# The spectrum of each kernel step as two row tiles of 64 rows, copied out in two halves, with a new order of the whole program

## The chip, the cores and the metric

The kernel runs on one core of one Trainium2 chip. The metric is the device time of one execution in microseconds (us), as a median over several executions. The engines of a core work side by side, each through its own instructions in a fixed order: TensorE (PE in the profile, with its weight loads as PEld), VectorE (DVE), ScalarE (ACT), GpSimd (POOL), and SyncE (SP), which issues most of the transfers.

## The reference

The reference runs two rounds of two layers on 2048 tokens of 512 channels. The first layer is a long convolution (S4D): from the parameters a kernel of 2048 taps is made for each channel, and the convolution is done by FFT. The second sends the two best-scored tokens through a feed-forward network. Cut to what matters here:

```python
def _A_ref(u, log_A_real, A_imag, C_real, C_imag, log_dt, D_skip):
    dt = jnp.exp(log_dt)
    A = -jnp.exp(log_A_real) + 1j * A_imag
    C = (C_real + 1j * C_imag) * dt[:, None]
    P = jnp.exp((A * dt[:, None])[:, :, None] * pos[None, None, :])
    K = 2.0 * jnp.einsum("dn,dnl->dl", C, P).real
    Kf = jnp.fft.rfft(K, L2)
    Uf = jnp.fft.rfft(u_t, L2)
    y = jnp.fft.irfft(Uf * Kf[None, :, :], L2)[:, :, :L]
    return y + u * D_skip[None, None, :]
...
    x = x + _A_ref(_layernorm(x, axis=-1), ...)
    x = x + _B_ref(_layernorm(x, axis=-1), ...)
    x = x + _A_ref(_layernorm(x, axis=-1), ...)
    x = x + _B_ref(_layernorm(x, axis=-1), ...)
```

## The kernel before

The 512 channels are cut into four chunks (c) of 128. The convolution kernel K of all channels is made in 32 steps u (class KStep), eight to a chunk, 16 channels to a step. The change touches the end of a step.

**One step.** ACT, POOL and DVE make the terms: ACT the phase and its sine and cosine (tiles ph and tr, lines 665, 693, 699 and 702), POOL the phase sums and the decay (ph and mg, lines 669, 683 and 688), DVE their products (sc, lines 710, 712 and 717). Then PE contracts them over the 128 states into the taps of the step (contract, L725, 32 matmuls in four column tiles of 32 columns): the tile pk has 128 partitions, 32 rows a for each of four channels g, and four such groups e. ACT copies pk to SBUF as kt (taps, L729), DVE adds the skip term (skip, L732). PE makes the first stage of the spectrum (spectrum, L745): for each e, kt is the stationary operand of two matmuls (real and imaginary part) against the constant d1k of 128 columns, 32 frequencies for each of four channels. d1k is block diagonal: it holds zeros where channel and row group differ. The result kq fills one PSUM bank, and ACT copies it out (turn, L755, 512 elements per partition) into gk, the spectrum tile of the chunk, laid out as 32 frequencies by 128 channels. The copy writes runs of four neighbouring channels.

**The PSUM banks.** pk and kq share one bank (tag "pk", one buffer) in turn: the contraction of the next step waits for the turn of the one before. The bank with tag "u" (one buffer) belongs to the convolution itself: to kx of even number (kf_mm, L778, second stage of the spectrum of K) and to pu (front_mm, L778, the same stage for the input), which two products on DVE read (front_tt, L819: p<-pu,kd and p<-pu,ks).

**The stages.** From about 20 us to 280 us (times of the profile) the 32 steps run, and interleaved with them the convolution of chunks 0 to 2 in the first round: zf (L845, first stage of the input), kx, pu, pv (back_mm, L827, first inverse stage), the copy w of pv on ACT (L1102), the way of w through DRAM (vd, then v) and po (L913, last stage). The copies on ACT differ in how they lie in memory: L498 copies 128 floats into every eighth place of the tile eight (32 bytes apart), L500 pairs of 16-bit halves into the same places, L641 writes exponentials into every second place (8 bytes apart) in the set-up, and L1693, late in the program, reads 512 floats that lie 128 bytes apart, with a factor per partition.

From 280 us on there are no steps any more: chunk 3, the routed tokens (pt, pi, pr, pq, ph, then pg and pu on the weights, L1470), the second round, and the routed tokens again at the very end (from 500 us).

**What sets the order.** Each call of the program (put_in) belongs to a lane, and the table PLAN gives every call of a lane its position in one agenda. The calls are sorted by that position, and each engine runs its instructions in the order in which they were then written. A second PLAN section orders what comes after 280 us. The lines "aw" (keep_awake, L1697) are matmuls whose result nobody reads; they keep PE going where it would sit idle.

Of the kernel before, what the change touches and what calls it, by code (L numbers as in the profile page):

```python
# [42 lines left out]
    ],  # L43
    x0=[103, 57, 141, 123],
    stat0=[105, 107, 104, 110, 99, 58, 59, 97, 161, 150, 144, 142, 128, 131, 124, 125],
    phase8=[
        94, 108, 109, 112, 85, 179, 199, 240, 259, 220, 346, 354, 364, 375, 358, 456, 470, 476, 492, 478, 606, 630, 631, 633, 589,
        707, 731, 782, 783, 791, 907, 933, 934, 946, 896, 1055, 1078, 1081, 1082, 1057,
    ],
    decay8=[  # L50
        87, 117, 121, 126, 106, 207, 247, 266, 277, 214, 371, 389, 390, 391, 393, 466, 474, 505, 509, 511, 601, 602, 603, 638,
        627, 740, 774, 775, 777, 727, 901, 929, 950, 960, 895, 1095, 1096, 1100, 1108, 1161,
    ],
    phase_0=[
        114, 113, 166, 152, 260, 264, 304, 330, 376, 407, 406, 445, 493, 538, 577, 518, 647, 676, 702, 690, 784, 787, 865, 815,
        947, 970, 1020, 1033, 1133, 1165, 1225, 1085,
    ],
# [19 lines left out]
    ],  # L77
    prod_b=[
# [3 lines left out]
    ],  # L82
    prod_p=[
# [3 lines left out]
    ],  # L87
    contract=[
        140, 209, 237, 271, 316, 348, 367, 384, 420, 463, 501, 529, 565, 598, 654, 670, 715, 721, 764, 831, 871, 930, 964, 980,
        997, 1073, 1125, 1175, 1230, 1246, 1275, 1286,  # L90
    ],
    z=[153, 481, 751, 1065],
    table=[162, 163, 168, 173, 174, 180, 181, 189, 190, 191, 193, 194, 430],
    taps=[
        164, 210, 243, 278, 324, 349, 368, 386, 423, 464, 506, 531, 578, 618, 655, 671, 716, 733, 770, 849, 876, 931, 966, 981,
        1013, 1089, 1127, 1178, 1231, 1247, 1277, 1287,
    ],
    skip=[
        182, 211, 248, 281, 325, 350, 373, 388, 431, 471, 507, 542, 585, 619, 657, 672, 717, 734, 771, 860, 883, 936, 967, 988,
        1015, 1090, 1129, 1189, 1236, 1252, 1278, 1293,  # L100
    ],
    spectrum=[
        183, 230, 298, 301, 334, 355, 381, 400, 450, 489, 508, 543, 637, 649, 662, 681, 754, 951, 816, 861, 903, 941, 975, 989,
        1068, 1107, 1150, 1241, 1255, 1267, 1300, 1318,
    ],
    keep=[184, 226, 249, 282, 347, 353, 374, 432],
    turn=[
        195, 231, 300, 309, 335, 365, 383, 401, 453, 490, 521, 546, 643, 650, 663, 685, 755, 958, 817, 862, 908, 948, 976, 990,
        1072, 1112, 1152, 1242, 1256, 1273, 1307, 1320,
    ],  # L110
    norm=[
# [15 lines left out]
    params=[340, 469, 520, 684, 893, 1006],
    inv=[359],
# [1738 lines left out]
```

## Time and profile before

| | us |
|---|---|
| median of three runs | 533.95 |
| lowest and highest | 530.01 and 534.79 |
| the profiled execution | 535.15 |
| its span, first to last instruction | 533.3 |

Busy time in the profiled execution: PE 437.0 us, DVE 424.5, ACT 386.3, POOL 316.9. The profile cuts the span into stages; busy time per stage is to be read against the length of the stage. The end of a matmul is modelled, so PE's busy time is not PE at its peak. A duration is that of one instruction from start to end; instructions that follow each other on one engine overlap a little, so the distance from one start to the next is what an instruction costs an engine that is never idle. The trace puts an idle time before an instruction down to what ended it (`<-`).

### The profile page before, as it was taken

Reading aid. Unit: us, or ns where it says so; the run is one execution under the profiler, and the core shown is the slowest. Engines: PE = TensorE matmul, PEld = TensorE weight load, DVE = VectorE, ACT = ScalarE, POOL = GpSimd, SP = SyncE. Lnnn points to the kernel's source line nnn. Section 1 sums busy time; section 2 is a strip of 40 time slices with the busy share of each in tenths; the row PEclk is TensorE's granted clock in tenths of the full one; section 3 lists DMA queues with packets and bytes.
Section 4 is the critical chain, followed back from the end, with each engine's and each line's share of the span. In section 5 each row is a group of like instructions: output and inputs, shape, how many; then the busy total and the mean of one; then the engine's idle time right before and its main releaser. Section 6 shows DMA issues by size and latency. Waiting matters only on the chain. (4 is left out here: it accounts for less than half of the span.)

```text
span 533.3 us, 14085 instructions
## 1 busy us (share of the span) xinstructions
PE 437.0 (82%) x5428; PEld 341.9 (64%) x5428; DVE 424.5 (80%) x987; ACT 386.3 (72%) x862; POOL 316.9 (59%) x334
## 2 busy tenths in 40 slices
PE   1014378999999999989989985999799999989468
PEld 1013356889778887779749743766578798754235
DVE  7999987878989998999885588574457799799841
ACT  5998989999998998888714645143556867559891
POOL 0496679997978487554506824056306868987200
PEclk9999999999999999999999998799899999999769
DMA  7244988879576877767636899743574668747643
GB/s 252 98 178 132 278 310 305 250 178 256 160 214 172 222 224 249 212 142 218 198 123 197 303 398 361 292 166 116 152 268 157 192 185 256 224 163 329 237 178 140
DMA packets 67307, 115.77 MB, mean 217 GB/s; under 512 B 8708, under 2 KB 50984, under 8 KB 62504
## 3 DMA queue, kind: packets, MB, share of 16 engines
q1 hardware_dynamic: 67112, 114.85, 66.0%
q8 instruction: 43, 0.70, 0.5%
q14 instruction: 24, 0.20, 0.1%
q0 software_dynamic: 128, 0.02, 0.0%
HBM read 68.83 MB, written 39.72 MB: 204 GB/s over the span
## 5 line engine op out<-in xcount | busy, mean ns | idle before, releaser
L873 POOL TENSOR_TENSOR y<-p 64x256 f32<-64x256 f32 x76 | 58.3, 768 | 73.4 <-DVE p L858 56.6
L717 DVE TENSOR_TENSOR sc<-tr,mg 128x1024 f32<-128x1024 f32 x64 | 77.1, 1210 | 2.1 <-POOL mg L688 1.5
L725 PE MATMUL pk<-sc 128*32 128x64 f32 x2048 | 39.6, 235 | 36.6 <-DVE sc L717 28.1
L725 PEld LDWEIGHTS pk<-sc 128*32 128x32 f32 x2048 | 34.1, 119 | 47.8 <-issue 29.1
L669 POOL TENSOR_TENSOR ph<-eight,far 128x768 int32<-128x768 int32 x32 | 53.3, 1672 | 16.2 <-ACT tr L702 15.8
L845 PE MATMUL zf<-z,d 128*128 128x256 f32 x192 | 57.8, 438 | 0.2 <-DVE b L1412 0.2
L683 POOL TENSOR_TENSOR mg<-eight,far 128x768 f32<-128x768 f32 x32 | 53.5, 1672 | 7.0 <-DVE sc L712 6.3
L849 DVE STREAM_TRANSPOSE g<-zf 128x512 f32<-128x512 f32 x64 | 45.0, 709 | 15.9 <-PE zf L845 14.6
L745 PE MATMUL kq<-d1k,kt 128*64 128x128 f32 x512 | 38.5, 297 | 16.7 <-ACT rq0b L949 9.2
L1102 ACT ACTIVATE w<-pv 128x512 f32<-128x512 f32 x48 | 28.2, 590 | 32.7 <-PE pv L879 18.7
L879 PE MATMUL pv<-y,w 128*128 128x128 f32 x320 | 46.1, 286 | 4.7 <-POOL y L871 3.0
L688 POOL TENSOR_TENSOR mg<-mg,f32s 128x512 f32<-128x512 f32 x32 | 34.2, 1071 | 24.4 <-ACT mg L677 16.6
L879 PEld LDWEIGHTS pv<-y,w 128*128 128x128 f32 x320 | 39.7, 191 | 13.5 <-POOL y L871 5.1
L858 DVE TENSOR_TENSOR p<-pu,kf 128x1024 f32<-128x1024 f32 x32 | 38.9, 1222 | 10.2 <-PE pu L768 5.8
L745 PEld LDWEIGHTS kq<-d1k,kt 128*64 128x64 f32 x512 | 30.2, 147 | 24.8 <-ACT rq0b L949 9.4
L845 PEld LDWEIGHTS zf<-z,d 128*128 128x128 f32 x192 | 37.6, 213 | 11.2 <-DVE g L849 2.5
L768 PE MATMUL pu<-g,w 128*64 128x128 f32 x640 | 43.1, 278 | 0.4 <-DVE b L1449 0.3
L768 PEld LDWEIGHTS pu<-g,w 128*64 128x64 f32 x640 | 36.8, 134 | 7.1 <-issue 4.3
L871 POOL TENSOR_TENSOR y<-p 64x256 f32<-64x256 f32 x52 | 38.6, 743 | 3.2
L827 PE MATMUL pv<-p,w 128*128 128x128 f32 x192 | 38.2, 280 | 0.0
L827 PE MATMUL pv<-p,w3b 128*128 128x128 f32 x192 | 37.1, 275 | 0.0
L702 ACT ACTIVATE tr<-ph,cst 128x1024 f32<-128x1024 f32 x32 | 35.6, 1113 | 1.5 <-DVE sc L717 1.0
(380 smaller groups left out, 1138.5 us busy)
## 6 DMA issues: line engine op xcount, KB each, us to landing
vd<-w SPq DMA_DIRECT2D x48, 256.0 KB, 3.0
v<-vd SPq DMA_DIRECT2D x24, 512.0 KB, 5.7
wd<-in_wd SPq DMA_DIRECT2D x4, 2048.0 KB, 11.0
kf<-kfd SPq DMA_DIRECT2D x16, 512.0 KB, 6.7
ks<-kd SPq DMA_DIRECT2D x48, 128.0 KB, 2.8
kfd<-kd SPq DMA_DIRECT2D x24, 256.0 KB, 3.7
x<-in_xr SPq DMA_DIRECT2D x4, 1024.0 KB, 6.4
z<-in_x SPq DMA_DIRECT2D x4, 1024.0 KB, 5.4
```

The lines of the kernel that those rows point to most:

```text
L669: G.tensor_tensor(self.ph[:, :, 8:32].rearrange("p d (k i) -> p d k i", k=3), self.first(0).rearrange("p d (o i) -> p d o i", o=1).to_broa ...
L683: G.tensor_tensor(mg[:, :, 0:2, 8:32].rearrange("p d t (k i) -> p d t k i", k=3), self.first(1).rearrange("p (d t o) i -> p d t o i", t=2, ...
L717: V.tensor_tensor(sc.rearrange("p d (t i) -> p d t i", t=3)[:, :, 0:3:2, :], t, self.mg[:, :, 0:3:2, :], op=OP.mult)
L725: T.matmul(self.pk[32 * g : 32 * g + 32, e, :], t[:, 0:32], t[:, 32:96], start=k == 1, stop=k == 0, tile_position=(0, 32 * g))
L745: T.matmul(self.pq[64 * ri : 64 * ri + 64, e].rearrange("p k g -> p (k g)"), self.kt[:, e].rearrange("p h b -> p (h b)"), d1k[:, 128 * ri ...
L768: T.matmul(pt[64 * par : 64 * par + 64, ri, q, :], w2[:, k1, 64 * ri : 64 * ri + 64], col(src, k1), start=True, stop=True, tile_position=( ...
L827: T.matmul(pv[:, k, :], w[:, j, :], p[:, t, k % 2, k // 2, :], start=t == 0, stop=t == 1)
L845: T.matmul(pf[:, 16 * s : 16 * s + 16, :], d1[:, 128 * s : 128 * s + 128], z[:, :, 16 * q : 16 * q + 16], start=True, stop=True)
L849: V.transpose(g[:, :, 16 * q : 16 * q + 16, :].rearrange("p k e t -> p e k t"), pf.rearrange("p (k t) e -> p e k t", t=2))
L858: V.tensor_tensor(pp, pu.rearrange("p (o r) q e -> p o r (q e)", o=1).to_broadcast([128, 2, 2, 2 * CH]), kf.rearrange("p r (o q) e -> p r ...
L873: E.tensor_tensor(y[0:64, :, par, :], p[0][ls, 0], p[1][ls, 1], op=OP.subtract)
L879: T.matmul(pv[:, k, :], w3[:, 4 * gi + k, :], y[:, k // 2, k % 2, :], start=True, stop=True)
```

## The change

1. The spectrum is cut in two by rows. Rows 0 to 63 of kt (channels g = 0, 1) and rows 64 to 127 (g = 2, 3) are multiplied apart, each against 64 columns of d1k, which is 128 columns wide now and has lost half of its zeros. A step has 16 matmuls of 64 rows, 64 stationary and 64 moving columns, in place of 8 of 128 rows, 64 stationary and 128 moving columns.
2. The two row tiles write to different banks: the first to the bank of pk as before, the second to the bank "u".
3. The turn becomes two instructions on ACT, one for each half, of 256 elements per partition. The channels of a step are dealt to e and g in another way (contract and the layout of the skip term follow), so that a half covers eight neighbouring channels; the copy runs over the 32 frequencies innermost, and in gk neighbouring frequencies lie 128 floats apart. It therefore writes single floats 512 bytes apart.
4. The store of the taps of chunk 0 (keep) is two transfers in place of one, eight times.
5. The tables of PLAN are all new, also those of the stages after 280 us. No other instruction is added or removed, but ACT has 21 loads of its function tables in place of 20; the additional one stands in the set-up, before step 2.

```diff
@@ constants
-    d1k = np.zeros((4, 32, 2, 32, 4))
+    d1k = np.zeros((4, 32, 2, 2, 32))
     for g in range(4):
-        d1k[g, :, 0, :, g] = np.cos(th)
-        d1k[g, :, 1, :, g] = -np.sin(th)
+        d1k[g, :, 0, g % 2, :] = np.cos(th)
+        d1k[g, :, 1, g % 2, :] = -np.sin(th)
@@ contract
-                            t = self.sc[:, k, 4 * e + g, :]
+                            t = self.sc[:, k, 8 * (g // 2) + 2 * e + g % 2, :]
@@ spectrum
-                self.pq = psk.tile([128, 4, 32, 4], F32, name=f"kq{self.u}", tag="pk")
+                self.pq = [
+                    (ps if r else psk).tile([128, 4, 2, 32], F32, name=f"kq{self.u}_{r}", tag=("pk", "u")[r]) for r in range(2)
+                ]
                 for e in range(4):
-                    for ri in range(2):
-                        T.matmul(
-                            self.pq[64 * ri : 64 * ri + 64, e].rearrange("p k g -> p (k g)"),
-                            self.kt[:, e].rearrange("p h b -> p (h b)"),
-                            d1k[:, 128 * ri : 128 * ri + 128],
-                            start=True, stop=True, tile_position=(0, 64 * ri),
-                        )
+                    for r in range(2):
+                        for ri in range(2):
+                            T.matmul(
+                                self.pq[r][64 * ri : 64 * ri + 64, e].rearrange("p g k -> p (g k)"),
+                                self.kt[64 * r : 64 * r + 64, e].rearrange("p h b -> p (h b)"),
+                                d1k[64 * r : 64 * r + 64, 64 * ri : 64 * ri + 64],
+                                start=True, stop=True, tile_position=(64 * r, 64 * ri),
+                            )
@@ turn
-            def turn(self):
-                if self.s == 0:
+            def turn(self, r):
+                if self.s == 0 and gks.get(self.c) is None:
                     gks[self.c] = new_big(f"gk{self.c}", "C")
-                A.activation(
-                    gks[self.c][:, :, 16 * self.s : 16 * self.s + 16].rearrange("p k (e g) -> p e k g", g=4),
-                    self.pq, AF.Copy)
+                at = 16 * self.s + 8 * r
+                A.activation(gks[self.c][:, :, at : at + 8].rearrange("p k e -> p e k"), self.pq[r].rearrange("p e g k -> p (e g) k"), AF.Copy)
@@ PLAN (one line of many)
-    first=[12, 62],
+    first=[12, 69],
```

In what follows, the number behind a tile's name is its step or its place (kq9 is the spectrum of step 9, kq9_0 and kq9_1 its halves, pu0_0_1 the input's second stage of chunk 0, group 1); the last number is a buffer's. On PE at steps 9 and 10, before:

```order
L745 MATMUL kq9_1201<-d1k_93,kt9_1152 64x128 x8
L778 MATMUL pu0_0_1_1218<-g0_0_705,w2_63 128x128 x4
L725 MATMUL pk10_1229<-sc10_1101 32x64 x32
L827 MATMUL pv0_0_1_1265<-p0_0_1_1226,w3_810 128x128
L827 MATMUL pv0_0_1_1265<-p0_0_1_1226,w3b_811 128x128
L827 MATMUL pv0_0_1_1265<-p0_0_1_1226,w3_810 128x128
L827 MATMUL pv0_0_1_1265<-p0_0_1_1226,w3b_811 128x128
L827 MATMUL pv0_0_1_1265<-p0_0_1_1226,w3_810 128x128
L827 MATMUL pv0_0_1_1265<-p0_0_1_1226,w3b_811 128x128
L827 MATMUL pv0_0_1_1265<-p0_0_1_1226,w3_810 128x128
L827 MATMUL pv0_0_1_1265<-p0_0_1_1226,w3b_811 128x128
L745 MATMUL kq10_1278<-d1k_93,kt10_1275 64x128 x8
```

On PE at the same place, with the change:

```order
L751 MATMUL kq9_0_1296<-d1k_93,kt9_1254 64x64 x2
L751 MATMUL kq9_1_1297<-d1k_93,kt9_1254 64x64 x2
L751 MATMUL kq9_0_1296<-d1k_93,kt9_1254 64x64 x2
L751 MATMUL kq9_1_1297<-d1k_93,kt9_1254 64x64 x2
L783 MATMUL pu0_0_1_1317<-g0_0_708,w2_63 128x128 x4
L726 MATMUL pk10_1327<-sc10_1145 32x64 x32
L751 MATMUL kq10_0_1369<-d1k_93,kt10_1366 64x64 x2
L751 MATMUL kq10_1_1370<-d1k_93,kt10_1366 64x64 x2
```

Before, eight matmuls of pv stood between the contraction pk10 and the spectrum kq10; now kq10 follows pk10 at once, and pu0_0_1, which follows kq9, writes the bank that kq9_1 holds. On ACT at the same steps, before:

```order
L1102 ACTIVATE w0_0_0_1197<-pv0_0_0_1174 128x512
L755 ACTIVATE gk1_1099<-kq9_1201 128x4x32x4
L838 ACTIVATE z0_1_1188<-z0_1_1188,bz0_105,rs0_104 128x128
L665 ACTIVATE ph12_1213<-eight0_3_1104 128x32x16
L702 ACTIVATE tr2_11_1262<-ph11_1077,cst_68 128x1024
L729 ACTIVATE kt10_1275<-pk10_1229 128x256
```

On ACT at the same steps, with the change:

```order
L1107 ACTIVATE w0_0_0_1293<-pv0_0_0_1269 128x512
L762 ACTIVATE gk1_1192<-kq9_1_1297 128x8x32
L762 ACTIVATE gk1_1192<-kq9_0_1296 128x8x32
L703 ACTIVATE tr2_11_1325<-ph11_1207,cst_68 128x1024
L843 ACTIVATE z0_1_1129<-z0_1_1129,bz0_105,rs0_104 128x128
L666 ACTIVATE ph12_1364<-eight0_3_1282 128x32x16
L730 ACTIVATE kt10_1366<-pk10_1327 128x256
```

One instruction has become two, and the second half, from the bank "u", is copied out first; the neighbours on ACT are the same kinds as before. On PE at the end of the program, where the routed tokens lead to the weights pg, before:

```order
L1420 MATMUL pr1_6038<-b1_14_6012,sm_66 8x1 x2
L1437 MATMUL pq1_6062<-b1_23_6053,sm_66 8x32 x2
L1461 MATMUL ph1_6082<-b1_25_6068,b1_26_6069 128x8
L1462 MATMUL ph1_6082<-b1_25_6068,b1_19_6035 128x8
L1470 MATMUL pg1_6087<-wgu_3667,b1_4_5911 32x448 x16
```

On PE at the same place, with the change:

```order
L1426 MATMUL pr1_6357<-b1_14_6315,sm_66 8x1 x2
L1703 MATMUL aw1_6370<-d1_64,sm_66 128x256
L1703 MATMUL aw1_6374<-d1_64,sm_66 128x256
L1703 MATMUL aw1_6382<-d1_64,sm_66 128x256
L1443 MATMUL pq1_6384<-b1_23_6365,sm_66 8x32 x2
L1703 MATMUL aw1_6393<-d1_64,sm_66 128x256
L1467 MATMUL ph1_6397<-b1_25_6390,b1_26_6391 128x8
L1468 MATMUL ph1_6397<-b1_25_6390,b1_19_6354 128x8
L1476 MATMUL pg1_6415<-wgu_3995,b1_4_6204 32x448 x16
```

Three keep-awake matmuls have moved in behind pr and one behind pq, where none stood before; the total number of them is the same.

## Rows read from the trace of the kernel before

**Rows 1.** The first lines of the page: the span, and the busy time of each engine over the whole span with its share and its number of instructions.

```profile
span 533.3 us, 14085 instructions
PE 437.0 (82%) x5428; PEld 341.9 (64%) x5428; DVE 424.5 (80%) x987; ACT 386.3 (72%) x862; POOL 316.9 (59%) x334
```

**Rows 2.** Busy time by stretch. Columns: the stretch, its length, the busy time of PE, PEld, DVE, ACT and POOL with the number of instructions, the clock granted to PE (1.00 is full speed), the share of the transfer engines, GB/s.

```profile
20.00:60.00 40.00, 9.76 (x224) 8.30 (x224) 38.84 (x67) 37.16 (x62) 33.45 (x29) 1.00 0.52 177
110.00:256.00 146.00, 141.84 (x2200) 122.58 (x2196) 130.70 (x257) 128.64 (x223) 105.53 (x92) 1.00 0.73 203
20.00:180.00 160.00, 119.62 (x2067) 102.88 (x2068) 142.19 (x235) 149.68 (x253) 131.21 (x114) 1.00 0.72 220
100.00:160.00 60.00, 58.70 (x1003) 51.19 (x1002) 50.47 (x78) 57.54 (x101) 51.78 (x48) 1.00 0.75 204
20.00:260.00 240.00, 196.31 (x3212) 168.10 (x3212) 215.02 (x394) 215.86 (x366) 182.41 (x158) 1.00 0.72 213
260.00:280.00 20.00, 17.92 (x300) 10.71 (x298) 17.31 (x53) 8.45 (x14) 1.06 (x1) 1.00 0.53 181
```

**Rows 3.** Whom PE waited for between 78 and 236 us, the same columns: the whole answer.

```profile
PE kq L745 <- DVE kt L732: 2.1, 3, 0.7
PE pk L725 <- ACT gk L755: 1.4, 2, 1.2
PE pu L778 <- DVE p L819: 1.1, 2, 0.7
PE po L913 <- DMA v<-vd: 0.5, 1, 0.5
PE pk L725 <- DVE sc L712: 0.3, 1, 0.3
```

**Rows 4.** PE in order of time, around steps 9 and 10: start, duration, instruction, and in brackets the idle time before it and what ended it.

```profile
109.08 1.09 PE L745 MATMUL kq<-d1k,kt 128*64 128x128 f32 x16
110.10 1.17 PE L778 MATMUL pu<-g,w 128*128 128x128 f32 x8
111.43 1.10 PE L725 MATMUL pk<-sc 128*32 128x64 f32 x64 [0.15 <-ACT gk L755]
112.46 0.49 PE L827 MATMUL pv<-p,w 128*128 128x128 f32 x2
```

**Rows 5.** Busy time by stretch of the spectrum alone (L745): PE and PEld with the number of instructions, then clock and transfers as in rows 2. Some records of PE stand twice or are missing; PEld counts 272.

```profile
110.00:256.00 146.00, 18.78 (x276) 14.50 (x272) 1.00 0.73 203
```

**Rows 6.** PE in order of time, two contractions early in the program that stand behind a turn.

```profile
48.46 1.94 PE L725 MATMUL pk<-sc 128*32 128x64 f32 x64 [1.02 <-ACT gk L755]
54.90 1.94 PE L725 MATMUL pk<-sc 128*32 128x64 f32 x64 [1.81 <-ACT gk L755]
```

**Rows 7.** Groups of instructions on ACT, shapes apart: line, operation, output<-input, shapes, count | busy us, mean ns of one | idle time before.

```profile
L755 ACT ACTIVATE gk<-kq 128x512 f32<-128x512 f32 x32 | 18.8, 588 | 8.1 <-PE kq L745 7.9
L729 ACT ACTIVATE kt<-pk 128x256 f32<-128x256 f32 x32 | 12.1, 377 | 10.4 <-PE pk L725 10.2
L641 ACT ACTIVATE su<-su 128x128 f32<-128x128 f32 x6 | 1.8, 309 | 1.8 <-DVE su L606 1.8
L498 ACT ACTIVATE eight<-near 128x128 f32<-128x128 f32 x6 | 2.6, 438 | 0.0
L1693 ACT ACTIVATE lt<-kw,b 128x512 f32 x8 | 9.3, 1190 | 9.9 <-PE po L910 6.5 <-DVE b L1609 3.4
L641 ACT ACT_TABLE_LOAD x4 | 5.1, 1283 | 0.1
```

**Rows 8.** ACT in order of time, start and duration.

```profile
103.92 0.59 ACT L755 ACTIVATE gk<-kq 128x512 f32<-128x512 f32 x1
104.39 0.44 ACT L500 ACTIVATE eight<-near 128x256 int16<-128x256 int16 x1
...
106.53 0.39 ACT L729 ACTIVATE kt<-pk 128x256 f32<-128x256 f32 x1
106.79 0.46 ACT L498 ACTIVATE eight<-near 128x128 f32<-128x128 f32 x1
107.01 1.16 ACT L699 ACTIVATE tr<-ph 128x1024 f32<-128x1024 int32 x1
```

**Rows 9.** Busy time by stretch of the turn alone (L755): the stretch, its length, busy time of ACT with the number of turns, then clock and transfers as in rows 2.

```profile
20.00:260.00 240.00, 15.84 (x27) 1.00 0.72 213
110.00:256.00 146.00, 10.59 (x18) 1.00 0.73 203
```

**Rows 10.** Whom ACT waited for between 20 and 260 us: us in total, times, longest.

```profile
ACT w L1102 <- PE pv L827: 7.3, 12, 1.8
ACT gk L755 <- PE kq L745: 3.3, 6, 1.3
ACT kt L729 <- PE pk L725: 3.0, 7, 0.7
```

**Rows 11.** Pieces of the chain that ended last, in order of time: the weights of the routed tokens in the first round and at the end.

```profile
347.40 3.13 PE pg L1470 x30
350.54 3.08 PE pu L1470 x62
...
513.14 5.75 PE pg L1470 x32
518.89 3.03 PE pu L1470 x64
```

**Rows 12.** Busy time by stretch around those two (columns as in rows 2).

```profile
347.00:351.00 4.00, 4.00 (x58) 1.66 (x58) 3.78 (x8) 1.44 (x4) 2.34 (x3) 1.00 1.00 415
513.00:519.00 6.00, 5.86 (x40) 1.97 (x44) 1.79 (x7) 5.63 (x15) 0.00 (x0) 0.56 0.81 326
```

More of the change, by code (lines that the diff above doesn't have):

```diff
@@ new lines @@
+    x0=[75, 57, 144, 104],
+    stat0=[102, 108, 103, 106, 99, 100, 60, 98, 167, 146, 149, 145, 126, 122, 118, 117],
+    decay8=[
+        115, 127, 128, 129, 76, 219, 220, 222, 285, 284, 385, 396, 398, 401, 387, 483, 484, 487, 488, 534, 615, 619, 630, 631,
+        618, 769, 774, 775, 805, 770, 914, 928, 948, 950, 970, 1085, 1086, 1088, 1090, 1171,
+    ],
+    phase8=[
+        91, 110, 111, 112, 89, 183, 184, 185, 186, 217, 359, 360, 361, 363, 365, 489, 490, 492, 493, 482, 607, 657, 658, 659, 647,
+        779, 788, 800, 801, 812, 912, 936, 937, 943, 888, 1078, 1080, 1132, 1133, 1092,
@@ L100 @@
-        1015, 1090, 1129, 1189, 1236, 1252, 1278, 1293,
+        168, 228, 255, 291, 335, 356, 381, 400, 456, 478, 512, 554, 590, 617, 670, 683, 734, 758, 794, 849, 910, 965, 992, 1009,
+        1059, 1105, 1153, 1218, 1265, 1279, 1305, 1320,
     ],
+    table=[170, 171, 172, 173, 174, 195, 196, 197, 198, 203, 204, 205, 455],
     spectrum=[
-        183, 230, 298, 301, 334, 355, 381, 400, 450, 489, 508, 543, 637, 649, 662, 681, 754, 951, 816, 861, 903, 941, 975, 989,
-        1068, 1107, 1150, 1241, 1255, 1267, 1300, 1318,
+        187, 229, 257, 307, 348, 367, 382, 411, 457, 498, 513, 559, 639, 651, 674, 690, 768, 974, 840, 884, 923, 966, 993, 1012,
+        1126, 1249, 1173, 1268, 1285, 1294, 1334, 1341,
@@ L136 @@
+    front_mm=[
+        463, 502, 479, 529, 547, 570, 591, 600, 785, 796, 811, 830, 851, 865, 900, 929, 1087, 1107, 1143, 1163, 1185, 1194, 1205,
+        1223,
+    ],
+    front_tt=[
+        464, 473, 507, 508, 480, 481, 531, 532, 550, 551, 572, 576, 596, 597, 620, 622, 786, 787, 798, 807, 821, 822, 832, 833,
+        854, 855, 873, 874, 905, 906, 930, 934, 1094, 1095, 1108, 1113, 1144, 1145, 1164, 1165, 1186, 1187, 1196, 1201, 1216,
+        1217, 1235, 1237,
     ],
     kf_sw=[
-        416, 485, 419, 494, 515, 550, 563, 610, 697, 712, 778, 792, 821, 836, 864, 859, 1074, 1102, 1075, 1111, 1142, 1144, 1174,
@@ new lines @@
+    e_mm=[3, 15, 33, 18, 47, 58, 65, 68],
+    e_kcp=[4, 14, 25, 28, 23, 60, 67, 70],
+    e_tt=[5, 16, 34, 29, 48, 62, 71, 86],
+    e_y=[
+        6, 12, 8, 10, 19, 21, 20, 26, 42, 43, 44, 45, 37, 39, 40, 38, 54, 56, 63, 55, 74, 76, 77, 75, 78, 81, 80, 79, 89, 90, 94,
+        91,
+    ],
+    e_w=[7, 192, 9, 241, 247, 221, 165, 82],
+    e_kst=[17, 97, 253, 438],
+    e_i1=[32, 36, 59, 50, 69, 83, 85, 95],
+    e_v=[41, 61, 66, 53, 88, 84, 87, 96],
+    r2_w=[
+        1100, 116, 1172, 1007, 1074, 1164, 1059, 224, 1170, 51, 1163, 1078, 1167, 235, 432, 410, 1097, 427, 915, 1019, 1110, 1173,
+        93, 1165, 377, 1107, 142, 1052,
+    ],
@@ new lines @@
+    e_f0=[92, 73, 99, 98, 72, 131, 137, 100],
+    e_ft=[101, 111, 108, 104, 107, 119, 118, 135],
+    e_fm=[102, 114, 112, 105, 109, 133, 138, 148],
+    e_fb=[103, 115, 113, 106, 110, 134, 139, 154],
+    e_wd=[117, 182],
+    e_hs=[
+        144, 122, 123, 140, 132, 147, 130, 151, 127, 125, 168, 121, 180, 136, 120, 126, 167, 169, 171, 159, 155, 157, 181, 164,
+        158, 170, 161, 160, 172, 163, 178, 173,
+    ],
+    e_ma=[149, 124, 143, 177, 150, 176, 166, 162, 153, 141, 183, 145, 184, 152, 174, 190],
@@ new lines @@
+    e_hm=[128, 175, 198, 199],
+    e_hd=[129, 179, 204, 200],
+    t_kf=[244, 146, 299, 350, 312, 506, 414, 458, 617, 616, 576, 520, 762, 797, 688, 861],
+    r1_w=[503, 237, 287, 220, 187, 188, 201, 384, 1171, 156],
+    r1=[
[4 rows of a table added]
+    ],
+    t_sq=[189],
+    r1_tab=[217, 218, 222, 223, 225, 226, 227, 228, 229, 230],
+    r1_z=[231],
+    r1_n=[251, 257, 256, 250, 234, 248, 255, 232, 233, 254, 240, 259, 258, 249, 239, 252],
+    e_st=[236],
+    r1_fa=[260, 274, 282, 268, 276, 261, 283, 272],
+    r1_fb=[264, 275, 284, 270, 278, 266, 286, 273],
@@ L288 @@
+    t_dm=[615, 583, 568, 715, 962, 959, 1029, 930, 935, 933, 950, 920],
+    t_ds=[830, 683, 611, 807, 1028, 975, 1044, 931, 951, 949, 953, 929],
+    e_sq=[620],
+    t_f0=[922, 934, 925, 940, 945, 918, 979, 927],
+    t_ft=[936, 932, 941, 943, 946, 948, 954, 956],
+    t_fm=[938, 937, 942, 944, 947, 955, 980, 987],
+    t_fb=[957, 939, 952, 958, 968, 984, 982, 988],
+    t_hm=[960, 1026, 1027, 1035],
     t_hs=[
-        956, 967, 971, 962, 964, 1015, 983, 970, 987, 1006, 957, 975, 980, 960, 961, 966, 1021, 1027, 1026, 998, 1012, 1028, 995,
@@ L378, in constants @@
         d1=d1.reshape(128, 256).astype(f),
-        d1k=d1k.reshape(128, 256).astype(f),
+        d1k=d1k.reshape(128, 128).astype(f),
         d4=np.stack([d4.reshape(128, 64), d4.reshape(4, 32, 64).transpose(1, 0, 2).reshape(128, 64)], 1).astype(f),
@@ L449, in build @@
         ps = kpctx.enter_context(tc.tile_pool(name="ps0", bufs=1, space=PSUM))
-        d1k = kp.tile([128, 256], F32, name="d1k", tag="d1k")
+        d1k = kp.tile([128, 128], F32, name="d1k", tag="d1k")
         dskt = kp.tile([128, 32, 4], F32, name="dskt", tag="dskt")
@@ L752, in turn @@
-            def turn(self):
-                if self.s == 0:
+                    for r in range(2):
+                        for ri in range(2):
[5 more added lines that the diff above has]
+                            )
@@ L1240, in build @@
                 put_in("keep", k.keep)
-            put_in("turn", k.turn)
+            for r in range(2):
+                put_in("turn", k.turn, r)
         run()
```

243 lines of the change are left out of this document (92 added, 151 removed), and 83 rows, old and new, of tables (decay, norm, out, prod_b).

## Prediction

> **What bounds the kernel now.** The page's first lines, PE busy 82% of the span and DVE 80% [rows 1], average over stages with different limits, so I read the busy time by stretch first. The steps run from about 20 to 280 us. Up to 60 us DVE is busy 38.84 of 40 us and ACT 37.16, while PE does 9.76 us of work [rows 2]: the set-up and the first steps are bound by DVE and ACT. From 110 to 256 us PE is busy 141.84 of 146 us [rows 2], and in the list of PE's waits between 78 and 236 us every entry together makes 5.4 us [rows 3]: there PE is the bound. The reader is to see a second thing in the same rows. ACT is not far behind. From 20 to 180 us it is busy 149.68 of 160 us, 93.5%, and at its densest, from 100 to 160 us, 57.54 of 60, 95.9%; over 20 to 260 us it is busy 215.86 of 240 us, 90% [rows 2]. So a change that takes work from PE and gives work to ACT has little room. After 260 us ACT is loaded lightly, 8.45 of 20 us [rows 2].
>
> **PE: the spectrum.** In the order of time a spectrum stands at 109.08 and the next matmul at 110.10: it costs PE 1.02 us for 16 matmuls in two column tiles. A contraction stands at 111.43 and the next at 112.46: 1.03 us for 64 matmuls of 64 columns in four column tiles, 16 ns from start to start [rows 4]. The new spectrum has 32 matmuls of 64 columns in four tiles (two by rows, two by columns). If row tiles overlap as column tiles do, it costs 32 x 16 = 0.52 us, 0.5 us less than before; if they don't, it costs 1.03 us as now. No matmul of the trace has a row tile behind the first, so both are bounds; I take 0.52, since the contraction is the nearest in form. Between 110 and 256 us there are 272/16 = 17 spectra [rows 5], so PE has 8.5 us less to do there. [...]
>
> **PE: the hand-overs.** Part of this is given back. The second half of kq sits in the bank "u", so a pu behind a spectrum now waits until ACT has copied that half out: kq9 then pu0_0_1 in the order of PE. And kq10 stands right behind pk10, without the pv that covered the way over ACT and DVE. In the new order I count seven places between steps 8 and 25 where pu or pk follows a spectrum at once. What such a wait costs the early contractions show, which stand behind a turn with little between: 1.02 and 1.81 us [rows 6]. With the dense order before, the same wait came to 1.4 us in all [rows 3]. Seven times 1.0 is 7 us as the upper bound, 1.4 us as the lower; I take 4 us. So PE's own balance from 110 to 256 us is 8.5 - 4 = 4.5 us less.
>
> **ACT: the turn.** One copy of 512 elements takes 588 ns and one of 256 from PSUM 377 ns [rows 7]. With nothing else, two halves are 754 ns. But they write single floats 512 bytes apart, where the old turn wrote runs of four. The nearest row is the copy at L498, which writes 128 single floats 32 bytes apart and takes 438 ns; activations that write 128 floats 8 bytes apart take 309 (L641) [rows 7]. That is 129 ns for 128 elements, 1.0 ns each. In the order of time the cost shows in the next instruction: L498 starts at 106.79, the next at 107.01, and that one takes 1.16 us [rows 8]. A second row is L1693, which reads 512 single floats 128 bytes apart: 1190 ns, 2.3 ns an element [rows 7]. So a half takes 377 + 256 = 633 ns, or 595 by L1693's 2.3 ns. Two halves cost 0.60 to 0.68 us more than the one; an instruction more on ACT also overlaps its neighbour by about 0.1 us (a turn of 0.59 us is followed after 0.47 [rows 8]), so I take +0.57 us a step. The lower bound, if the stride costs nothing, is 2 x 0.377 - 0.588 - 0.1 = +0.07.
>
> [...]
>
> **ACT: the sum.** 27 turns lie between 20 and 260 us [rows 9]: 27 x 0.57 = 15.4 us. The additional table load takes 1.28 us [rows 7] and stands in the set-up, where ACT has 2.8 us of idle time in 40 [rows 2]. Together 16.7 us, so ACT's work in that stretch grows from 215.9 to 232.6 us. Where ACT is full, it reaches 93.5 to 95.9% [rows 2]; at these rates the work needs 248.8 to 242.5 us in place of 240: 2.5 to 8.8 us more. I take 4.5, nearer to the lower end, because 13.6 us of ACT's idle time there were waits for PE [rows 10], and PE is done earlier now. PE's gain doesn't come off this: ACT, not PE, ends the stretch.
>
> **The rest.** The eight additional transfers of keep and the smaller d1k come early, where PE idles: nothing. After 280 us the instructions are the same and only their order is new; I see one place with a price. [...] Before, PE had nothing but tiny matmuls between pr and pg; now four keep-awake matmuls stand there. If they keep the clock up, 2.6 us are won; I count half, 1.3. For the other moves I take nothing, with 2 us either way.
>
> **The sum.** The profiled execution took 535.15 us. 535.15 + 4.5 - 1.3 = 538.4. The median of the runs shown is 533.95, 1.2 us below the profiled one; against it I forecast 537.
>
> **The rivals.** The forecast, chance 0.49: ACT bounds the stretch, 533 to 543, likeliest 537.
>
> First, the strided copy is free, 0.17. Then ACT gets 27 x 0.07 + 1.28 = 3.2 us more and stays at 91%, and PE remains the bound with its balance of -4.5: 533.95 - 4.5 - 1.3 = 528. For it speaks that the old turn, which jumps 512 bytes after every run of four, is as quick as its length of 512 lets one expect from the 377 ns for 256 [rows 7]; against it speaks L498.
>
> Second, ACT takes the work into its gaps, 0.16. If it reaches 232.6 of 240 us, 97%, the stretch keeps its length: 533.95 - 1.3 = 532.7. Against it: in none of the stretches read is ACT above 95.9% [rows 2].
>
> Third, PE stalls on the bank "u", 0.18. If the row tiles don't overlap, the spectrum is no shorter; the seven waits of 1.0 us and ACT's 4.5 us add up to 533.95 + 7 + 4.5 = 545. It decides from a spectrum of about 0.8 us on, where PE's gain of 17 x 0.2 = 3.4 us is less than the waits.
>
> **How the numbers follow.** Differences below about 1%, 5.3 us, cannot be told from none here. Faster than 528.6: 0.10 of the first rival's 0.17, and 0.06 from the lower ends of the second and of the forecast, 0.16. Slower than 539.3: 0.15 of the third rival's 0.18, and of the forecast, whose upper half reaches past that line, 0.21: 0.36. Between: 0.48. The range takes in the free copy below (526) and the stalls above (547).
>
> **What would show it.** The turn's row: 128x256 with 600 to 640 ns (380 would be the first rival). Spectrum to next start on PE: 0.5 us. ACT busy 20 to 260 us at 95% or more, PE's busy share from 110 to 256 us down from 97% to some 90%, with waits for the turn. pg at the end at 3.1 or 5.7 us. Wrong would be the forecast if the turn is at 380 ns, or if ACT stays below 92% and the steps still end later.

## The result, and the profile after

The changed kernel took 533.78 us (median of 18 runs, 530.5 to 540.97), the kernel before, run beside it, 531.45 us (median of 18 runs, 528.68 to 535.68): ratio 1.0058, 95% interval 1.0033 to 1.0082. By the medians that is 2.3 us more, within the 1% that counts as no change; the forecast was 537 against 533.95, 3.1 us more. The two profiled executions alone would tell the opposite, 533.16 us after and 535.15 before. One execution differs from the next by some us, so prices below come from medians, and from a trace only what it shows of an instruction, a wait or a stretch. Ratios compare each kernel's executions near its fastest; in the last group of runs the kernel before had two at 523.93 and 524.59 us, which lift all four ratios of that group.

The page's first lines after, which answer to [rows 1]:

```profile
span 531.0 us, 15165 instructions
PE 422.6 (80%) x5940; PEld 329.5 (62%) x5940; DVE 422.9 (80%) x987; ACT 399.4 (75%) x895; POOL 315.7 (59%) x334
```

Busy time by stretch after, which answers to [rows 2] and, in the last line, to [rows 12]; columns as there:

```profile
20.00:60.00 40.00, 8.07 (x256) 7.00 (x256) 36.31 (x64) 38.22 (x65) 31.48 (x29) 1.00 0.61 219
110.00:256.00 146.00, 135.08 (x2451) 115.74 (x2451) 129.28 (x252) 134.40 (x237) 106.42 (x95) 1.00 0.70 201
20.00:260.00 240.00, 182.79 (x3522) 155.50 (x3523) 211.64 (x390) 224.23 (x389) 177.40 (x156) 1.00 0.68 209
513.00:519.00 6.00, 6.00 (x96) 3.77 (x88) 1.54 (x6) 6.00 (x16) 0.00 (x0) 1.00 0.80 322
```

From 110 to 256 us PE is busy 135.08 us where it was 141.84, and ACT 134.40 where it was 128.64: the work has gone from the one to the other, and now neither is full. ACT reaches 224.23 of 240 us, 93.4%. Over the whole span ACT's busy time grows by 399.4 - 386.3 = 13.1 us.

The groups of the two copies on ACT after (columns as in [rows 7]), and PE in order of time around a spectrum with other work behind it (columns as in [rows 4]):

```profile
L762 ACT ACTIVATE gk<-kq 128x256 f32<-128x256 f32 x64 | 36.6, 627 | 8.7 <-PE kq L751 8.4
L730 ACT ACTIVATE kt<-pk 128x256 f32<-128x256 f32 x32 | 12.2, 382 | 6.7 <-PE pk L726 6.5
```

```profile
141.60 0.69 PE L751 MATMUL kq<-d1k,kt 64*64 64x64 f32 x32
142.23 1.13 PE L850 MATMUL zf<-z,d 128*128 128x256 f32 x4
```

Both copies move 256 elements out of PSUM; the one that writes single floats 512 bytes apart takes 627 ns, the other 382. The spectrum takes 0.63 us to the next start, where it took 1.02. (The trace has two instructions for each of these fp32 matmuls, so the 16 of a step are 32 in it; from here on the spectrum's matmuls are counted as in the trace, as in the prediction.)

A duration is not what the copy costs ACT. A half in order of time, with the instruction behind it:

```profile
144.23 0.64 ACT L762 ACTIVATE gk<-kq 128x256 f32<-128x256 f32 x1
144.63 0.45 ACT L678 ACTIVATE mg<-eight 128x256 f32<-128x256 f32 x1
```

The next instruction starts 0.40 us after the half, 0.24 before the half ends. Two halves side by side cost about 0.85 us from start to start; the one copy before cost 0.47 [rows 8].

Whom PE waited for between 78 and 236 us (us in total, times, longest), which answers to [rows 3]:

```profile
PE pk L726 <- ACT gk L762: 3.4, 5, 0.7
PE kq L751 <- DVE kt L733: 2.9, 5, 0.9
PE pu L783 <- ACT gk L762: 2.8, 4, 1.2
PE pk L726 <- issue: 1.6, 2, 1.4
PE zf L850 <- DVE g L854: 1.3, 2, 0.8
```

The waits for the turn, pk's and pu's, were 1.4 us and are 3.4 + 2.8 = 6.2 us. DVE's wait for pu there, before and after:

```profile
DVE p L819 <- PE pu L778: 2.5, 5, 1.5
...
DVE p L824 <- PE pu L783: 6.1, 8, 2.4
```

And the matmuls of the last pg, first to last start, with the durations' minimum, median and maximum:

```profile
L1476 PE MATMUL pg<-wgu,b x32: 536/539/564, 512.3 to 515.0; 128*32 128x448 f32 x32
```

In [rows 11] this pg took 5.75 us, at a mean granted clock of 0.56 [rows 12]; now it takes 3.2 us, at 1.00.

### The profile page after: what moved, and what is told of

Same layout as the page of the kernel before. It is cut to its first block, busy times and chain, and to the rows that moved or that the text cites. A ratio compares the mean times of both kernels' runs of the same rounds, so it can differ in the third digit from the quotient of the medians.

```text
span 531.0 us, 15165 instructions
## 1 busy us (share of the span) xinstructions
PE 422.6 (80%) x5940; PEld 329.5 (62%) x5940; DVE 422.9 (80%) x987; ACT 399.4 (75%) x895; POOL 315.7 (59%) x334
## 5 line engine op out<-in xcount | busy, mean ns | idle before, releaser
L850 PE MATMUL zf<-z,d 128*128 128x256 f32 x192 | 55.9, 426 | 6.0 <-ACT z L843 3.2
L1107 ACT ACTIVATE w<-pv 128x512 f32<-128x512 f32 x48 | 28.3, 592 | 27.7 <-PE pv L884 17.2
L850 PEld LDWEIGHTS zf<-z,d 128*128 128x128 f32 x192 | 36.2, 207 | 15.8 <-ACT z L843 3.5
L762 ACT ACTIVATE gk<-kq 128x256 f32<-128x256 f32 x64 | 36.6, 627 | 8.7 <-PE kq L751 8.4
L751 PE MATMUL kq<-d1k,kt 64*64 64x64 f32 x1024 | 25.8, 239 | 21.6 <-DVE kt L733 19.7
L751 PEld LDWEIGHTS kq<-d1k,kt 64*64 64x64 f32 x1024 | 20.8, 146 | 30.7 <-DVE kt L733 24.6
```

The costliest lines, as they stand in the source:

```text
L751: T.matmul(self.pq[r][64 * ri : 64 * ri + 64, e].rearrange("p g k -> p (g k)"), self.kt[64 * r : 64 * r + 64, e].rearrange("p h b -> p (h ...
L850: T.matmul(pf[:, 16 * s : 16 * s + 16, :], d1[:, 128 * s : 128 * s + 128], z[:, :, 16 * q : 16 * q + 16], start=True, stop=True)
```

## The experiments

The theories: **A**, my forecast's: ACT's doubled, strided copy ends the steps. **B**: the hand-overs of bank "u" on PE do. **C**: the new order itself costs. B came back as **D** for the order of before, and **E** asked whether the parts add up. All results in one table; the diffs below it are cut to the lines that carry the change. "Median" is the kernel's, with the difference to the median of the kernel before that ran beside it; "x loaded" is the start of the transfer x<-xs behind the first routed round, a point at the same place of the program in all of them, give or take a matmul of keep-awake and of pv, and "pg" the duration of the last pg, both from the profiled execution.

| kernel | median, us | ratio, 95% interval | x loaded | pg |
|---|---|---|---|---|
| before (profile ahead) | | | 369.90 | 5.75 |
| changed | 533.78, +2.3 | 1.0058, 1.0033 to 1.0082 | 372.28 | 3.2 |
| changed, runs of two | 530.73, -1.3 | 0.9977, 0.9932 to 1.0022 | 368.41 | 5.0 |
| new order alone | 534.27, +2.2 | 1.0063, 1.0033 to 1.0094 | 371.13 | 4.7 |
| new code in the order of before | 553.66, +21.6 | 1.0434, 1.0373 to 1.0494 | 390.1 | 5.6 |
| changed, without row tiles | 540.5, +8.4 | 1.0175, 1.012 to 1.0229 | 378.18 | 4.8 |
| new code, runs of two, order of before | 549.9, +17.6 | 1.0346, 1.0293 to 1.0399 | 387.2 | 5.6 |
| before with ACT's two halves | 536.69, +4.4 | 1.0115, 1.0064 to 1.0165 | 371.00 | 5.1 |
| runs of two, ten more keep-awake | 530.78, -1.5 | 1.0007, 0.9964 to 1.005 | 366.49 | 3.2 |
| changed, runs of eight | 530.63, -1.7 | 0.994, 0.9895 to 0.9985 | 370.85 | 4.5 |
| new order, ACT's two halves, one bank | 542.47, +10.5 | 1.0289, 1.0221 to 1.0357 | 381.8 | 4.6 |
| before, four keep-awake moved | 533.54, +1.6 | 1.0085, 1.0031 to 1.0139 | 367.88 | 5.1 |
| runs of eight, ten more keep-awake | 531.33, -0.6 | 1.0069, 1.0018 to 1.0119 | 368.51 | 4.8 |
| changed, once more | 534.09, +2.1 | 1.0122, 1.0043 to 1.02 | 373.26 | 3.2 |

The last four rows are the last group: their ratios stand beside 1.0122 for the changed kernel itself, which had 1.0058 before.

**Runs of two floats.** The columns of d1k change places, so that a half writes two neighbouring floats at a time:

```diff
-    d1k = np.zeros((4, 32, 2, 2, 32))
+    d1k = np.zeros((4, 32, 2, 32, 2))
-                A.activation(gks[self.c][:, :, at : at + 8].rearrange("p k e -> p e k"), self.pq[r].rearrange("p e g k -> p (e g) k"), AF.Copy)
+                A.activation(gks[self.c][:, :, at : at + 8].rearrange("p k (e g) -> p e k g", g=2), self.pq[r], AF.Copy)
```

> The changed kernel, but each half writes runs of two floats (8 bytes) 512 bytes apart instead of single floats. Theory A (ACT's doubled, strided copy ends the steps): a half falls from 627 ns to 380-400 ns if two neighbouring floats are enough, 27 x 2 x 0.24 = 13 us less for ACT between 20 and 260 us, the last turn ends about 4 to 6 us earlier and the time is about 4 to 6 us below that of the changed kernel, 1.0 to 0.99 of before. If a run of two isn't enough the half stays above 550 ns and nothing moves. Theory B (hand-overs of bank u on PE): the half may fall, the time stays within 1 us of the changed kernel. Theory C (the new order itself): as B.

The group of the turn on ACT in this kernel:

```profile
L762 ACT ACTIVATE gk<-kq 128x256 f32<-128x256 f32 x64 | 23.0, 390 | 10.2 <-PE kq L751 9.7
```

A half falls from 627 to 390 ns, and the time by 3.6 us against the changed kernel (from +2.3 to -1.3): just under what A said, and more than B and C allowed. ACT's busy time over the span falls from 399.4 to 390.6 us, 8.8 us or 0.28 us a step. So the strided write is a cost, and it reaches the end.

**The new order alone.** The kernel before with the new PLAN; of each pair of turn positions the first is used:

```diff
+PLAN["turn"] = PLAN["turn"][0::2]
```

> The kernel before with the new order alone: one bank, one turn of 588 ns, 16 matmuls of 128 rows. Theory A: the steps end as in the kernel before or a little earlier (-3 to +1 us), the last pg runs at 3.1-3.2 us instead of 5.75, so the time is 2 to 5 us below before (0.99 to 0.996). Theory B: the same. Theory C (the order costs): the steps end later as in the changed kernel, the time is 0 to 3 us above before in spite of the pg at the end.

It costs 2.2 us without any of the new code. A said 2 to 5 us less and is wrong here; C is right, for this part. The additional table load on ACT comes with the order: this kernel has it. So do most of the longer waits, PE's, DVE's and ACT's between 78 and 236 us:

```profile
PE pk L727 <- ACT gk L757: 3.5, 5, 0.7
...
DVE p L821 <- PE pu L780: 6.3, 9, 2.4
...
ACT gk L757 <- PE kq L747: 8.2, 13, 1.3
```

Before they were 1.4, 2.5 and 3.3 us. An order made for other instructions is no neutral ground, but it is the order that the new code runs in.

**The new code in the order of before.** PLAN of before, the two halves side by side, and five positions shifted, where bank "u" is in use in that order:

```diff
+PLAN["turn"][10] = 518.5
+PLAN["spectrum"][11], PLAN["turn"][11] = 556.3, 556.6
+PLAN["spectrum"][19], PLAN["turn"][19] = 863.3, 863.6
+PLAN["turn"][20] = 904.5
+PLAN["spectrum"][24], PLAN["turn"][24] = 1061.3, 1061.6
+PLAN["turn"] = [p for p in PLAN["turn"] for _ in range(2)]
```

> The changed code in the order of before, with the two halves of a turn side by side where the one turn stood. Theory A: the steps end 4 to 8 us later than before (a half at 627 ns), the last pg stays at 5.7 us, so the time is 4 to 8 us above before (1.008 to 1.015). Theory B: also later, and then PE's waits of pu, pk on a turn grow to 7 us or more between 78 and 236 us, where the changed kernel has 6.4. Theory C (the new order is what costs): 0 to 2 us above before.

It costs 21.6 us, far more than any theory said. PE, ACT and DVE of this kernel in order of time, around one spectrum:

```profile
132.37 0.69 PE L756 MATMUL kq<-d1k,kt 64*64 64x64 f32 x32
132.64 0.40 ACT L683 ACTIVATE mg<-eight 128x256 f32<-128x256 f32 x1
133.10 1.05 ACT L767 ACTIVATE gk<-kq 128x256 f32<-128x256 f32 x2
133.94 0.63 ACT L1112 ACTIVATE w<-pv 128x512 f32<-128x512 f32 x1
134.20 1.18 PE L788 MATMUL pu<-g,w 128*128 128x128 f32 x8 [1.13 <-ACT gk L767]
134.47 1.25 ACT L848 ACTIVATE z<-z,bz,rs 128x128 f32<-128x128 f32 x3
135.31 1.10 PE L731 MATMUL pk<-sc 128*32 128x64 f32 x64
135.42 0.69 DVE L829 TENSOR_TENSOR p<-pu,kd 128x512 f32<-128x512 f32 x1 [3.35 <-PE pu L788]
```

The pu behind the spectrum needs bank "u", waits 1.13 us until both halves are copied out, and DVE, which needs that pu, stands idle for 3.35 us. Between 78 and 236 us that adds up to (waits of PE, then of DVE):

```profile
PE pu L788 <- ACT gk L767: 7.4, 6, 1.9
...
DVE p L829 <- PE pu L788: 17.3, 8, 3.3
```

Before, PE had no such wait of pu on a turn in that stretch [rows 3], and DVE's wait for pu there was 2.5 us.

**Without row tiles.** Each of the 32 matmuls has 128 rows and a d1k with zeros:

```diff
-                                self.kt[64 * r : 64 * r + 64, e].rearrange("p h b -> p (h b)"),
-                                d1k[64 * r : 64 * r + 64, 64 * ri : 64 * ri + 64],
-                                start=True, stop=True, tile_position=(64 * r, 64 * ri),
+                                self.kt[:, e].rearrange("p h b -> p (h b)"),
+                                d1k[:, 128 * ri + 64 * r : 128 * ri + 64 * r + 64],
+                                start=True, stop=True, tile_position=(0, 64 * ri),
```

> The changed kernel without row tiles: each of the 32 matmuls contracts over all 128 rows with a d1k that has zeros in it (128x256); banks, turns and order as in the changed kernel. The spectrum on PE goes from 0.63 us back to about 1.0 us, 0.4 x 17 = 6.8 us more for PE between 110 and 256 us. Theory A (ACT ends the steps, PE's saving is off the path): PE's busy time goes from 135 to 141 us, ACT's stays at 134, the time is within 2 us of the changed kernel. If PE still ends part of the steps: 3 to 7 us above the changed kernel (1.01 to 1.02 of before).

PE in order of time around a spectrum, and the first of those whom ACT waited for between 78 and 236 us:

```profile
144.02 1.15 PE L751 MATMUL kq<-d1k,kt 128*64 128x64 f32 x32
145.10 1.13 PE L850 MATMUL zf<-z,d 128*128 128x256 f32 x4
```

```profile
ACT gk L762 <- PE kq L751: 6.9, 14, 1.1
```

The same wait in the changed kernel:

```profile
ACT gk L762 <- PE kq L751: 2.2, 5, 0.7
```

The spectrum takes 1.08 us, 0.45 more, and the 17 of them between 110 and 256 us make 7.6 us; the time is 6.1 us longer than that of the changed kernel (+8.4 against +2.3). ACT waits 6.9 us for spectra, in the changed kernel 2.2. So PE's saving is not off the path: nearly all of it comes off the time, and "ACT, not PE, ends the stretch" is wrong.

**New code, runs of two, in the order of before:** both edits above together.

> The changed code in the order of before (as the code-only kernel, which took 1.043 of before), with runs of two floats in place of single ones, so that a half takes some 390 ns and not 628. Theory D (in the order of before it is the second half's bank u that costs: pu waits for a turn, and DVE for pu): the time falls by the price of the stride alone, some 4 to 6 us, to 1.031 to 1.036; PE's waits of pu on a turn, 7.4 us between 78 and 236 us, and DVE's waits for pu, 17.3 us, stay above 5 and 12. Theory A (ACT's doubled, strided copy is the cost in either order): most of the 23 us goes, 1.00 to 1.015.

17.6 us stay, as D said; the stride was worth 21.6 - 17.6 = 4.0 us, as in the new order. PE's waits of pu on a turn are 5.1 us, DVE's for pu 13.4. In this order the stride is the smaller part of the cost, and the waits for bank "u" stay.

**The kernel before with ACT's two halves.** Its own order, its 16 matmuls and its one bank; only the copy out is doubled and strided:

```diff
-    d1k = np.zeros((4, 32, 2, 32, 4))
+    d1k = np.zeros((4, 32, 2, 4, 32))
+                at = 16 * self.s + 8 * r
+                A.activation(gks[self.c][:, :, at : at + 8].rearrange("p k e -> p e k"), self.pq[:, 2 * r : 2 * r + 2].rearrange("p e g k -> p (e g) k"), AF.Copy)
+PLAN["turn"] = [p for p in PLAN["turn"] for _ in range(2)]
```

> The kernel before in its own order, with its own 16 matmuls of 128 rows into one bank, and only the copy out changed: two halves of 256 elements, each of single floats 512 bytes apart. Theory A: ACT has 27 x 0.6 = 16 us more to do and the steps end 2.5 to 8.8 us later: 1.005 to 1.016, or 1.043 if A alone explains the code-only kernel. Theory D: also 1.005 to 1.016, but with PE's waits of pu on a turn below 2 us between 78 and 236 us, so that the rest up to 1.043 belongs to the bank.

4.4 us more, a half at 631 ns, no wait of pu on a turn in the list. This is the ACT term of the forecast by itself, without the table load, and near its size, 4.5. But ACT's busy time grew by only 396.9 - 386.3 = 10.6 us, 0.33 us a step. The rest of the 21.6 us, 17.2, came with the second bank, the row tiles (which make it smaller), keep's two transfers and the five shifted positions. The waits point to the bank: DVE's for pu are 3.5 us here and 17.3 there. The shifts were not run alone, so that they cost nothing is not shown; but the turns of the two kernels part by another 5.7 us between steps 16 and 18, and no position there was shifted.

**Ten more keep-awake matmuls** ahead of the second round's pt, with runs of two:

```diff
-NWARM = 10, 28
+NWARM = 10, 38
+PLAN["r2_w"] += [1051.5] * 10
```

> The kernel with runs of two, and ten more keep-awake matmuls ahead of the second round's pt, where PE idles for 8.35 us: 10 x 0.74 = 7.4 us of work in that gap. If the clock then stays up until pg, the last pg takes 3.1 to 3.3 us in place of 4.95 and the time is 1.5 to 2.5 us below the kernel with runs of two, 0.993 to 0.995 of before. [...]

In the profile pg takes 3.2 us, but the 1.5 to 2.5 us don't come: the median is that of the kernel with runs of two (530.78 and 530.73). See also the last group.

**Runs of eight floats:** the changed kernel's bank, read in another order.

```diff
-                A.activation(gks[self.c][:, :, at : at + 8].rearrange("p k e -> p e k"), self.pq[r].rearrange("p e g k -> p (e g) k"), AF.Copy)
+                A.activation(gks[self.c][:, :, at : at + 8], self.pq[r].rearrange("p e g k -> p k (e g)"), AF.Copy)
```

> The changed kernel with the elements of a half taken in another order: it writes runs of eight floats and reads single floats 128 bytes apart from PSUM, where the changed kernel reads in a row and writes single floats. If only the write's jumps cost, a half takes 377 to 390 ns and the time is that of the kernel with runs of two (0.998 of before). If jumps cost on either side (as in the copy at L1693, which reads 512 single floats 128 bytes apart and takes 1190 ns), a half takes 595 to 640 ns and the time is that of the changed kernel (1.006).

The group of the turn:

```profile
L762 ACT ACTIVATE gk<-kq 128x256 f32<-128x256 f32 x64 | 22.5, 379 | 11.6 <-PE kq L751 11.2
```

379 ns, where L730's copy of 256 elements without jumps took 382: the jumps in reading PSUM cost nothing, those in writing were all of it. (L1693, which gave the forecast its 2.3 ns an element, reads SBUF and has a factor per partition; what makes it slow no run shows.) By the medians the time is 4.0 us below that of the changed kernel (from +2.3 to -1.7).

**The last group.** The new order with ACT's two halves in one bank (the edit of the copy out above, with the first of each pair of turn positions used twice):

> The new order with before's 16 matmuls into one bank, and the copy out in two halves of single floats, side by side. Against the kernel with the new order alone (1.0063) it adds ACT's term only; against the kernel without row tiles (1.0175), which has two banks, it lacks the second half in bank u. Theory E (the parts add up within the new order): 1.012 to 1.016, and the rest up to 1.0175, 1 to 3 us, is bank u. If ACT's term is the same with and without row tiles, 4.3 us as between the changed kernel and the one with runs of two, 1.0144. Rival: the parts don't add up, below 1.009 or above 1.018.

The parts don't add up as E had it: +10.5 us, 8.3 more than the new order alone, where the same edit cost 4.4 in the order of before. PE's waits of pk on a turn are 6.5 us in 8 times. With the second bank (the kernel without row tiles, +8.4, whose halves also stand apart) it is 2.1 us less, within what the intervals leave open: in the new order bank "u" costs nothing that can be told. (The two also differ in 32 matmuls of 64 columns for 16 of 128, 1.08 us for 1.02, and in keep's two transfers.)

The kernel before with four keep-awake matmuls moved behind the second round's pr:

```diff
+_w = PLAN["r2_w"]
+for _a, _b in ((1042, 1105), (1043, 1106), (1047, 1107), (1049, 1112.5)):
+    _w[_w.index(_a)] = _b
```

> The kernel before with four of its keep-awake matmuls of the end moved behind the second round's pr, as in the new order, and nothing else. If it is they that shorten the last pg: 3.2 to 4.9 us in place of 5.75 and 0.5 to 2.5 us less, 0.995 to 0.999. If it is something else of the new order: pg at 5.1 to 5.8 and 1.000.

pg at 5.1 us, no time won: nothing shows that these four matmuls by themselves keep the clock up.

Runs of eight and ten more keep-awake together:

> The changed kernel with runs of eight floats written (a half took 379 ns) and ten more keep-awake matmuls ahead of the second round's pt. If the two add up as far as they were measured: 0.992 to 0.998 of before, the last pg at 3.2 us. If the keep-awake matmuls bring nothing: that of the kernel with runs of eight, 0.994 to 0.997, with pg at 4.5 or more in some executions.

pg at 4.8 us; 2.8 us below the changed kernel beside it, by the medians, less than the 3.6 to 4.0 us of the turn alone. The keep-awake matmuls bring nothing that can be told.

The changed kernel once more:

> The changed kernel once more, on the chip of the three kernels beside it and against the same runs of the kernel before: 1.003 to 1.008 again. Its profile shows what one execution differs from another: the last turn within 2 us of 285.3, a half at 627 ns, and a last pg anywhere between 3.2 and 5.0 us.

The last turn ends at 283.48 us where it ended at 285.33, within 2 us, while x is loaded 1 us later; neither mark of a single profile is exact to better than 1 to 2 us. A half takes 626 ns, pg 3.2 us. Against the kernel before, by medians, +2.1 us; before that +2.3. The ratio, 1.0122, lies above the 1.003 to 1.008 expected, in the lifted group.

## Why the prediction held, and what in it was wrong

The sum was right and three of its steps were not; that their errors cancel is luck. The chain of kernels in the new order shows it, each against the one ahead of it by the medians: new order alone +2.2; ACT's two strided halves in one bank +8.3; the second half in bank "u" -2.1; row tiles in place of 128 rows -6.1. Together +2.3. By the intervals the last three links are good to 3 to 5 us each, so the -2.1 is not told from nothing. The forecast had, against its own profile, +4.5 and -1.3.

- **The turn on ACT**, 595 to 633 ns: 627, right. The 0.57 us a step made of it was not: I took 0.1 us off for one overlap more, and each half overlaps its neighbour by some 0.2 us. ACT's busy time grew by 13.1 us, 1.3 of them the table load, so by 0.37 us a step. By the forecast's own way, 27 x 0.37 + 1.28 = 11.3 us make 227.1 us of work, and at 93.5 to 95.9% a stretch 3.2 us shorter to 2.9 longer. So the 4.5 us came from too much work, priced too low: it was 4.4 in the order of before, and in the new order the stride alone is worth 3.6 to 4.0 us, the whole edit 8.3 with one bank and 8.3 - 2.1 = 6.2 with two.
- **"PE's gain doesn't come off this: ACT, not PE, ends the stretch"** is the step that failed. I had read two busy shares, PE's 97% and ACT's 93.5 to 95.9%, and let the engine that the change fills decide alone. In this order the two wait for each other in turn, PE for the turn (6.2 us) and ACT for the spectrum (2.2 us, 6.9 without row tiles). Time taken from either came off: counted over the 17 steps from 110 to 256 us, 6.1 of 7.6 us on PE and 3.6 to 4.0 of 17 x 0.28 = 4.8 us on ACT.
- **The spectrum**, 0.52 us: 0.63, and 1.08 without row tiles, so the row tiles do overlap, at 20 ns from start to start instead of the contraction's 16. Mechanism right, saving 0.39 us a step in place of 0.5. The third rival's line of about 0.8 us is an estimate that 1.02 us, 17 spectra and 4 us of waits give, 1.02 - 4 / 17 = 0.78; 0.63 lies below it.
- **The hand-overs of bank "u"**, 4 us: PE's waits of pk and pu on a turn grew by 6.2 - 1.4 = 4.8 us between 78 and 236 us. Right in size; but pk's part of it comes with the order (3.5 us with the new order alone) and only pu's 2.8 us with the bank, in the new order one bank would have been no cheaper, and in the order of before the second came with some 17 us. There the wait of pu passes on to DVE. I had priced only PE's own idle time in it, 1.0 us a place.
- **"The rest", at nothing.** The new order by itself, table load included, costs 2.2 us where I counted -1.3, and it does so in the steps. From the load of x to the end of the span it is 163.4 us before (533.3 - 369.90), and 160.8 to 164.2, mean 162.1, in the five profiles with the order of before (one with the four matmuls moved); in the nine with the new order 158.7 to 160.5, mean 159.4. So the second half gains 2.7 us, and the first must lose that and 2.2 more; in the profiles x is loaded at 371.13 with the new order alone, against 369.90 and 367.88 (the kernel with the four matmuls moved, the same up to there), and what lacks lies within what one execution differs from the next. Of the gain, pg holds about 1.1 us: the five profiles with the order of before have it at 5.1 to 5.75, mean 5.4; seven with the new order, without more keep-awake, at 3.2 to 5.0, mean 4.3. The 2.6 of the forecast is the difference of the two pgs in [rows 11], 5.75 - 3.13, at mean granted clocks of 0.56 and 1.00 [rows 12]. My half of it was a fair size, but that four keep-awake matmuls win it no run shows: the kernel that moved only these had pg at 5.1. What shortens pg, and where the other 1.6 us of the second half come from, stays open. The waits that grow with the order alone are listed above; which move in it costs the steps their time stays open too.

Of the rivals: the first (the copy free) is what runs of two and of eight made of the kernel, and its price, 6 us below before, was too good, 1.3 and 1.7 came; the second (ACT at 97%) didn't happen, at 93.4%; the third's case, a spectrum no shorter, didn't happen, and the kernel without row tiles shows its price, 8.4 us where I had 11.5.

The version with runs of two or eight is 2.8 to 4.0 us below the changed kernel by the medians; against the kernel before it is 0.6 to 1.7 us lower, and of its four intervals one lies below 1, one above, in the lifted group, and two on both sides. So it undoes the loss; that it wins is not shown.

## What to carry to other kernels

When two engines are both above 90% in a stretch and wait for each other in a fixed order, price a change on each of them, by the distance from start to start and not by durations, and don't let one absorb the other's gain. A bank that is shared with another stage can cost what stands behind the stage that waits for it, here DVE's 17.3 us of waits behind PE's 7.4, so look for an order in which other work lies between. And when a copy has to jump, let it jump where it reads from PSUM and write in runs: here the same 256 elements cost 627 ns with the jumps in the write and 379 with those in the read.

## What the runs showed of the hardware

ACT's copy of 256 elements from PSUM to SBUF, by the run that it writes: single floats 627 to 638 ns, two floats 390, eight floats 379, the last with reads of single floats 128 bytes apart. So one jump of 512 bytes for a single float adds about 1 ns to the duration, (627 - 379) / 256, one for a run of two about 0.1 ns, (390 - 379) / 128, and the jumps of 128 bytes in reading PSUM nothing that shows: 379 ns with them, 382 for L730's copy without. Nearly half of the 1 ns is hidden under the next instruction: what ACT pays for the single floats is 8.8 us over 64 halves, 0.14 us a half or about 0.5 ns an element.

The clock at the end did not follow PE's work as I had thought. Busy time by stretch, of the kernel with runs of two and below it of the changed kernel (columns as in [rows 2]): a part of the pause ahead of pt, the matmuls from pi up to pg, and pg.

```profile
490.00:495.00 5.00, 0.00 (x0) 0.00 (x0) 4.53 (x26) 3.98 (x32) 1.42 (x2) 0.55 1.01 429
500.50:507.40 6.90, 6.43 (x28) 4.38 (x28) 4.25 (x21) 6.13 (x13) 0.92 (x1) 0.50 0.00 1
507.00:511.00 4.00, 3.65 (x21) 1.15 (x24) 2.15 (x9) 3.63 (x10) 0.00 (x0) 0.50 0.40 164
```

```profile
495.00:500.00 5.00, 0.00 (x0) 0.00 (x0) 4.64 (x29) 4.92 (x40) 2.36 (x2) 0.76 0.96 383
506.40:512.30 5.90, 5.39 (x28) 3.47 (x29) 4.16 (x22) 5.71 (x12) 0.92 (x1) 0.71 0.00 1
512.00:515.50 3.50, 3.17 (x36) 1.44 (x40) 2.15 (x9) 3.50 (x10) 0.00 (x0) 1.00 0.36 150
```

With the same instructions in the same order, PE is idle for 8.35 us ahead of pt in both kernels. Between pi and pg it is busy 6.43 of 6.9 us in the first and 5.39 of 5.9 us in the second, 93% and 91%; yet the first runs that stretch at a granted clock of 0.50 and starts pg so, and the second has a mean of 0.71 there and runs pg at 1.00. What PE did just ahead of pg doesn't tell the two apart. One profile of such a stretch shows one draw, not the price.
